# Running the first query block tile by tile at the head of a fused attention and gated-MLP kernel

**Chip, cores, metric.** One core of one Trainium2 chip. The metric is the device time of the program in microseconds (us); lower is better. Times are medians of several executions; most executions of one kernel agree within 0.3%. In the views PE is TensorE, PEld its weight loads, DVE VectorE, ACT ScalarE, and SPq the queue that issues DMAs; a block (or packet) of instructions is a piece of an engine's program that is fetched by DMA while the kernel runs.

## The reference

`x` is 2048 tokens by 512. Both branches read one layer-normalized `xn`, and the result is their sum with `x`.

```python
xn = (x - mean) / sqrt(var + 1e-5)
# A: sliding local attention, 32 heads of 16, a window of 8 keys two tokens apart
q, k, v = split(xn @ wqkv)
a = softmax(q . k[pos - 2*w] * 16**-0.5);  A = (sum_w a * v[pos - 2*w]) @ wo
# B: gated MLP with a spatial gate
z = gelu(xn @ w_in);  z1, z2 = z[:, :688], layernorm(z[:, 688:])
B = (z1 * (w_sp @ z2 + b_sp)) @ w_out
out = x + A + B
```

## The kernel before

Tokens come in 16 tiles of 128. Tile `i` belongs to block `i % 4`; block 0 is tiles 0, 4, 8, 12. To be of use to TensorE, a tile is loaded, its statistics taken on VectorE, the root on ScalarE, the tile normalized in place on VectorE, then transposed: by TensorE into PSUM and a copy (block 0, half of block 1) or by a DMA transpose (the rest). Below, "tile 0 to 3 of a block" counts within the block.

```python
load_x0(...); load_x(A, 0, 2, 4); load_wqk(SP, 0); load_x(SP, 1, 0, 2); load_wqk(SP, 1); ...   # all at the start

def ln_stats(i, parts=1):   # V.bn_stats, then V.bn_aggr
def ln_root(sl):            # A.activation(rstd, var, Abs_reciprocal_sqrt)
def ln_apply(i):            # V.tensor_scalar(x, x, mean, rstd, subtract, mult)

def tr(i):
    pt = ps_aux.tile([P, C, P], BF16, name="pt", tag="aux")          # four transposes in one PSUM tile
    for c in range(C):
        PE.transpose(pt[:, c, :], xall[:, j, tb, c * P:(c + 1) * P], ident[:])

def qk_part(pq, j, m, b0, b1, ccs=(0, 1), p0=None, kcs=range(C)):    # block j, tiles b0..b1 side by side
    for cc in ccs:
        for kc in kcs:
            PE.matmul(pq[:, cc, ...], wqk[:, sd, kc, c0 + cc:D:C], xv[:, kc, b0:b1, j, :],
                      start=(kc == 0), stop=(kc == C - 1))

# ---- prologue, cut
warm_up(10)
...                                            # tiles 0, 1 of block 0: statistics, roots, apply
tr_copy(t0[0], tr(t0[0]))
pt1 = tr(t0[1]); tr_copy(t0[1], pt1, 0, 2); tr_copy(t0[1], pt1, 2, 4)
warm_up(1); warm_up(1, 2)                      # filler matmuls
...                                            # tiles 2, 3: statistics, roots, then both applies
qk_part(pqs[0], 0, 0, 0, 2, kcs=range(2)) ...  # q, tiles 0 and 1 together, 256 columns a matmul
tr_copy(t0[2], tr(t0[2])) ...                  # tiles 2, 3: transposes
qk_part(pqs[0], 0, 0, 2, 4, ...) ...           # q, tiles 2 and 3 together
...                                            # k of block 0; tiles of block 1, two of them with tr_dma
load_x(SP, 3, 0, 4)
...                                            # q and k of block 1: first tiles 0 and 1, then tiles 2 and 3
ORDER = "z2.0 z1.3 p1.1 z2.2 zg2.0 p0.1 zg1.3 ..."   # the steady part, in a fixed order
```

The engines' orders are fixed by hand: each engine runs its instructions as the program names them.

Of the kernel before, what the change touches and what calls it, by code (L numbers as in the profile page):

```python
# [7 lines left out]
BF16 = mybir.dt.bfloat16  # L8
# [6 lines left out]
P = 128  # L15
S = 2048
D = 512
# [3 lines left out]
C = D // P  # L21
# [48 lines left out]
def kernel(  # L70
# [13 lines left out]
    V = nc.vector  # L84
    A = nc.scalar
    G = nc.gpsimd
    PE = nc.tensor
# [9 lines left out]
    ps_aux = ctx.enter_context(tc.tile_pool(name="ps_aux", bufs=2, space=PSUM))  # L97
# [4 lines left out]
    xall = r_x[:, 0:4 * TB * D].rearrange("p (j b d) -> p j b d", j=4, b=TB)  # L102
    vp = r_x[:].rearrange("p (d t) -> p d t", d=DH)
    r_w = sb.tile([P, 8192], BF16, name="r_w")
    wqk = r_w[:, 0:4096].rearrange("p (s k f) -> p s k f", s=2, k=C)
# [30 lines left out]
    xnT = sb.tile([P, C, S], BF16, name="xnT")  # L136
# [7 lines left out]
    ident = sb.tile([P, P], BF16, name="ident")  # L144
# [5 lines left out]
    stats = sb.tile([P, NT, 12], F32, name="stats")  # L150
# [21 lines left out]
    def load_x(E, j, b0, b1):  # L172
        for tb in range(b0, b1):
            E.dma_start(xall[:, j, tb], xblk[j][:, tb])
# [32 lines left out]
    def ln_stats(i, parts=1):  # L207
        j, tb = i % 4, i // 4
        w = D // parts
        for h in range(parts):  # L210
            V.bn_stats(stats[:, i, 6 * h:6 * h + 6], xall[:, j, tb, w * h:w * h + w])  # L211
        V.bn_aggr(mv[:, i, :], stats[:, i, 0:6 * parts])  # L212

    def ln_root(sl):
        A.activation(rstd[:, sl], mv[:, sl, 1], ACT.Abs_reciprocal_sqrt, bias=eps_t[:])

    def ln_apply(i):
        j, tb = i % 4, i // 4
        V.tensor_scalar(xall[:, j, tb, :], xall[:, j, tb, :], mv[:, i, 0:1], rstd[:, i:i + 1],  # L219
                        ALU.subtract, ALU.mult)  # L220

    def tr(i):
        j, tb = i % 4, i // 4
        pt = ps_aux.tile([P, C, P], BF16, name="pt", tag="aux")
        for c in range(C):
            PE.transpose(pt[:, c, :], xall[:, j, tb, c * P:(c + 1) * P], ident[:])
        return pt

    def tr_copy(i, pt, c0=0, c1=C):
        A.copy(xnT[:, c0:c1, i * P:(i + 1) * P], pt[:, c0:c1, :])  # L230

    def tr_copy_v(i, pt, c0, c1):
        V.tensor_copy(xnT[:, c0:c1, i * P:(i + 1) * P], pt[:, c0:c1, :])

    def tr_dma(i):
        j, tb = i % 4, i // 4
        SP.dma_start_transpose(xnT[:, :, i * P:(i + 1) * P], xall[:, j, tb, :])
# [57 lines left out]
    def qk_part(pq, j, m, b0, b1, ccs=(0, 1), p0=None, kcs=range(C)):  # L295
        sd, c0 = m // 2, 2 * (m % 2)
        p0 = b0 if p0 is None else p0
        xv = xnT[:].rearrange("p k (b j t) -> p k b j t", b=TB, j=4)
        for cc in ccs:
            for kc in kcs:  # L300
                PE.matmul(pq[:, cc, p0 * P:(p0 + b1 - b0) * P], wqk[:, sd, kc, c0 + cc:D:C],  # L301
                          xv[:, kc, b0:b1, j, :], start=(kc == 0), stop=(kc == C - 1))

    def qk_copy(pq, j, m, b0=0, b1=TB, p0=None):
        sd, c0 = m // 2, 2 * (m % 2)
        p0 = b0 if p0 is None else p0
        if sd == 0:
            dst = qs[:, j, c0:c0 + 2, b0 * P:b1 * P].rearrange("p c (b t) -> p c b t", b=b1 - b0)
        else:
            dst = ks[:, c0:c0 + 2, HALO:HALO + S].rearrange("p c (b j t) -> p c b j t", b=TB, j=4)[:, :, b0:b1, j, :]  # L310
        cast = A.copy(dst, pq[:, :, p0 * P:(p0 + b1 - b0) * P].rearrange("p c (b t) -> p c b t", b=b1 - b0))  # L311
        if sd == 1:
            for i in k_reads[j]:
                tc.declare_no_dep(cast.ins, i, reason="other token columns of the same rows")
            k_casts[j].append(cast.ins)

    def qk_tile():
        return ps_mm.tile([P, 2, TBS], F32, name="pq", tag="mm")

    def qk_mm(j, m):  # L320
        tiles["q", j, m] = qk_tile()
        qk_part(tiles["q", j, m], j, m, 0, TB)
# [220 lines left out]
    def blk(j):  # L543
        return [4 * tb + j for tb in range(TB)]

    def col(i):
        return slice(i, i + 1)
# [4 lines left out]
    def warm_up(n, b=4):  # L552
        for _ in range(n):
            PE.matmul(pwm[:, 0, 0:b * P].rearrange("p (a b) -> p a b", a=b), warm[:, 0:P],
                      warm[:, 0:P].unsqueeze(1).broadcast_to([P, b, P]), start=True, stop=True)

    t0, i1 = blk(0), blk(1)
    i2, i3 = blk(2), blk(3)
    warm_up(10)
    for n in range(2):  # L560
        ln_stats(t0[n], 2)
        ln_root(col(t0[n]))
    for n in range(2):
        ln_apply(t0[n])
    tr_copy(t0[0], tr(t0[0]))
    pt1 = tr(t0[1])
    tr_copy(t0[1], pt1, 0, 2)
    tr_copy(t0[1], pt1, 2, 4)
    warm_up(1)
    warm_up(1, 2)  # L570
    for n in range(2, 4):
        ln_stats(t0[n])
        ln_root(col(t0[n]))
    for n in range(2, 4):
        ln_apply(t0[n])
    pqs = [qk_tile() for _ in range(3)]
    qk_part(pqs[0], 0, 0, 0, 2, kcs=range(2))
    qk_part(pqs[0], 0, 0, 0, 2, kcs=range(2, 4))
    qk_part(pqs[1], 0, 1, 0, 2, (0,))
    tr_copy(t0[2], tr(t0[2]))  # L580
    qk_part(pqs[1], 0, 1, 0, 2, (1,), kcs=range(2))
    pt3 = tr(t0[3])
    qk_part(pqs[1], 0, 1, 0, 2, (1,), kcs=range(2, 4))
    tr_copy_v(t0[3], pt3, 0, 2)
    tr_copy(t0[3], pt3, 2, 4)
    qk_part(pqs[0], 0, 0, 2, 4, kcs=range(2))
    qk_part(pqs[0], 0, 0, 2, 4, kcs=range(2, 4))
    qk_part(pqs[1], 0, 1, 2, 4)
    ln_stats(i1[0])
    ln_root(col(i1[0]))  # L590
    ln_stats(i1[1])
    ln_root(col(i1[1]))
    qk_copy(pqs[0], 0, 0)
    ln_apply(i1[0])
    ln_apply(i1[1])
    qk_copy(pqs[1], 0, 1)
    qk_part(pqs[2], 0, 2, 0, 4)
    for n in range(2, 4):
        ln_stats(i1[n])
        ln_root(col(i1[n]))  # L600
    for n in range(2, 4):
        ln_apply(i1[n])
        tr_dma(i1[n])
    load_x(SP, 3, 0, 4)
    tr_copy(i1[0], tr(i1[0]))
    pq3 = qk_tile()
    qk_part(pq3, 0, 3, 0, 4, (0,))
    tr_copy(i1[1], tr(i1[1]))
    qk_part(pq3, 0, 3, 0, 4, (1,))
    qk_copy(pqs[2], 0, 2)  # L610
    qk_copy(pq3, 0, 3)
# [9 lines left out]
    pqs = [qk_tile() for _ in range(3)]  # L621
# [44 lines left out]
    for tok in ORDER.split():  # L666
        name = tok.rstrip("0123456789.")
# [31 lines left out]
```

## Time and profile before

| | before |
|---|---|
| median of 3 | 203.11 us (202.89 to 203.21) |
| profiled span | 201.2 us |
| TensorE busy | 196.0 us, 97% |
| TensorE's waits from 5 to 30 us | 0.5, 0.4 and 0.2 us |

The prediction shows the views of the kernel before, and reads them. Two lines more are wanted. The first is the chain of work that ended last, by engine; the second is from the timeline of VectorE, whose columns are start, length, engine, line, operation, output and input: its first product of q and k, with which the steady part begins.

```profile
PE 89%; DVE 5%; DMA 3%; ACT 1%; issue 1%
```

```profile
24.85 1.22 DVE L335 TENSOR_TENSOR r_pr<-r_qk 128x2048 bf16<-128x2048 bf16 x1
```

### The profile page before, as it was taken

What the parts mean: (1) busy time and instruction counts of PE and PEld (TensorE: products, weight loads), DVE (VectorE), ACT (ScalarE), POOL (GpSimd) and SP (SyncE); (2) the same over time, 40 slices, a digit from 0 to 9 for tenths busy, and PEclk for the clock granted to TensorE, in tenths of its full rate; (3) what the DMA queues carried; (4) which work ended last, traced back from release to release, by engine and by line L of the source; (5) the groups of instructions that cost most, each with busy time, mean ns of one, the idle gap of its engine ahead of it and who ended that gap; (6) DMA issues with size and microseconds to landing.
All of it is one profiled execution on the core that took longest, in us unless ns stands there. A gap on an engine that the chain in (4) does not pass through costs nothing.

```text
span 201.2 us, 4028 instructions
## 1 busy us (share of the span) xinstructions
PE 196.0 (97%) x1659; PEld 123.7 (62%) x1659; DVE 184.5 (92%) x248; ACT 104.5 (52%) x175; POOL 17.4 (9%) x14
## 2 busy tenths in 40 slices
PE   7898999999999999999999999999999999999994
PEld 2768855665566666666656666666544646664562
DVE  5896899999989999999979999999999999999715
ACT  3585998899999996363341513807502230331300
POOL 3000000499600000000000000000000000000000
PEclk9999999999999999999999999999999999999999
DMA  5977648980000095554266999199950199206864
GB/s 164 261 244 111 142 95 261 143 173 0 3 0 0 3 134 102 170 93 104 66 145 134 239 270 164 26 228 178 194 92 0 54 232 169 67 30 121 212 190 136
DMA packets 66562, 25.91 MB, mean 129 GB/s; under 512 B 56496, under 2 KB 66288, under 8 KB 66288
## 3 DMA queue, kind: packets, MB, share of 16 engines
q1 hardware_dynamic: 65824, 25.19, 58.5%
q10 hardware_dynamic: 720, 0.47, 0.7%
q8 instruction: 13, 0.21, 0.5%
q14 instruction: 5, 0.04, 0.1%
HBM read 10.13 MB, written 2.10 MB: 61 GB/s over the span
## 4 chain that ended last, share of the span: by engine, by line
PE 89%; DVE 5%; DMA 3%; ACT 1%; issue 1%
PE pg L444 37%; PE pz L243 19%; PE pq L301 10%; PE pv L405 7%; PE po L527 7%; PE po L497 6%; DVE stats L211 2%; DMA xnT<-r_x 2%; DMA r_x<-in_A_x_dram 1%; PE pa L527 1%; PE pl L355 1%; DVE r_pr L515 1%; PE po L506 1%; PE pb L497 1%; DVE r_x L219 1%; DVE mv L212 1%
## 5 line engine op out<-in xcount | busy, mean ns | idle before, releaser
L444 PE MATMUL pg<-z,r_qk 128*128 128x344 bf16 x448 | 66.8, 309 | 0.0
L444 PEld LDWEIGHTS <-r_qk 128*128 128x128 bf16 x448 | 43.7, 98 | 22.0 <-issue 0.4
L419 DVE TENSOR_TENSOR r_pr<-r_x,r_w 128x2048 bf16<-128x2048 bf16 x32 | 38.4, 1220 | 1.3 <-PE pl L355 1.0
L243 PE MATMUL pz<-w_z,xnT 128*128 128x344 bf16 x256 | 39.3, 310 | 0.0
L423 DVE TENSOR_TENSOR r_pr<-r_pr 128x2048 bf16<-128x2048 bf16 x28 | 33.9, 1219 | 0.8 <-DVE r_pr L423 0.5
L243 PEld LDWEIGHTS <-xnT 128*128 128x128 bf16 x256 | 24.9, 98 | 13.2 <-issue 0.4
L450 ACT ACTIVATE gs<-pg,b_col 128x688 bf16<-128x688 f32 x16 | 13.2, 833 | 35.4 <-PE pg L444 32.6
L301 PE MATMUL pq<-xnT,r_w 128*128 128x256 bf16 (+1 forms) x168 | 28.8, 324 | 0.8 <-DMA xnT<-r_x 0.5
L335 DVE TENSOR_TENSOR r_pr<-r_qk 128x2048 bf16<-128x2048 bf16 x24 | 27.8, 1218 | 0.5 <-ACT r_qk L311 0.5
L301 PEld LDWEIGHTS <-r_w 128*128 128x128 bf16 x176 | 19.2, 114 | 9.3 <-DMA xnT<-r_x 0.8
L641 POOL CAST b_col<-b 128x16 f32<-128x16 bf16 x1 | 15.4, 15356 | 35.1 <-DMA b<-in_B_b_sp_dram 35.1
L510 ACT CAST r_qk<-po 128x512 bf16<-128x512 f32 x10 | 5.6, 588 | 23.1 <-PE po L527 22.7
L311 ACT CAST r_qk<-pq 128x1024 bf16<-128x1024 f32 (+1 forms) x16 | 15.3, 986 | 3.2 <-PE pq L301 3.0
L292 ACT ACTIVATE r_uz<-pz 128x688 bf16<-128x688 f32 x16 | 11.7, 739 | 6.6 <-PE pz L243 6.5
L497 PE MATMUL po<-r_lg,r_pr 32*128 32x512 bf16 x192 | 14.5, 375 | 0.0
L405 PE MATMUL pv<-xnT,r_w 128*32 128x512 bf16 x256 | 14.2, 379 | 0.0
L527 PEld LDWEIGHTS <-r_uz 128*128 128x128 bf16 x85 | 8.0, 98 | 9.4 <-issue 1.1
L344 DVE TENSOR_TENSOR r_pr<-r_pr 128x4096 bf16<-128x4096 bf16 x6 | 13.7, 2286 | 0.0
L527 PE MATMUL po<-r_w,r_uz 128*128 128x512 bf16 x60 | 13.6, 380 | 0.0
L211 DVE BATCH_NORM_STATS2 stats<-r_x 128x6 f32<-128x512 bf16 (+1 forms) x18 | 10.8, 611 | 2.8 <-DMA r_x<-in_A_x_dram 2.8
L267 ACT ACTIVATE junk<-z 128x688 bf16<-128x688 bf16 x16 | 12.4, 774 | 0.1
L261 ACT ACTIVATE z<-pz 128x688 bf16<-128x688 f32 x16 | 11.8, 739 | 1.2 <-PE pz L243 1.2
(79 smaller groups left out, 185.2 us busy)
## 6 DMA issues: line engine op xcount, KB each, us to landing
r_lg<-in_A_wo_dram SPq DMA_DIRECT2D x8, 256.0 KB, 4.0
r_x<-in_A_x_dram SPq DMA_DIRECT2D x12, 128.0 KB, 3.1
out_dram<-r_qk SPq DMA_DIRECT2D x12, 128.0 KB, 3.6
r_w<-in_A_wqkv_dram SPq DMA_DIRECT2D x8, 128.0 KB, 3.5
r_qk<-in_A_x_dram SPq DMA_DIRECT2D x8, 128.0 KB, 2.5
w_z<-in_B_w_in_dram SPq DMA_DIRECT2D x4, 172.0 KB, 3.6
w_z<-in_B_w_in_dram SPq DMA_DIRECT2D x1, 688.0 KB, 6.9
r_w<-in_B_w_out_dram SPq DMA_DIRECT2D x1, 640.0 KB, 5.3
```

Of the source, the lines that this page charges most:

```text
L211: V.bn_stats(stats[:, i, 6 * h:6 * h + 6], xall[:, j, tb, w * h:w * h + w])
L243: PE.matmul(pz[:, hh, 0:FHALF], xnT[:, kc, i * P:(i + 1) * P], wz[:, kc, hh * FHALF:(hh + 1) * FHALF], start=(kc == 0), stop=(kc == C - 1))
L301: PE.matmul(pq[:, cc, p0 * P:(p0 + b1 - b0) * P], wqk[:, sd, kc, c0 + cc:D:C], xv[:, kc, b0:b1, j, :], start=(kc == 0), stop=(kc == C - 1))
L311: cast = A.copy(dst, pq[:, :, p0 * P:(p0 + b1 - b0) * P].rearrange("p c (b t) -> p c b t", b=b1 - b0))
L335: prod = V.tensor_tensor(pr[g % 3][:, c].rearrange("p w b t -> p b w t"), q3.unsqueeze(2).broadcast_to([P, TB, 4, P]), k4, ALU.mult)
L405: PE.matmul(pv[32 * tb:32 * tb + 32, dd, :], wv[:, kc, 2 * d2 + dd, :], xnT[:, kc, tb * TBS:(tb + 1) * TBS], start=(kc == 0), stop=(kc == ...
L419: V.tensor_tensor(pw_t[n], vp[:, :, off:off + P], a_sb[:, slot_w(w), ts].unsqueeze(1).broadcast_to([P, DH, P]), ALU.mult)
L423: V.tensor_tensor(pw_t[n] if dst is None else dst, pw_t[n], pw_t[m], ALU.add)
L444: PE.matmul(pg[:, hh, 0:FHALF], wsp[n][:, k, :], z2[:, k, hh * FHALF:(hh + 1) * FHALF], start=(k == 0), stop=(k == NT - 1))
L497: PE.matmul(pc, op[32 * tb:32 * tb + 32, d, o * P:(o + 1) * P], wo_r[32 * tb:32 * tb + 32, d, cs], start=(d == 8), stop=False, tile_positi ...
L527: PE.matmul(pc, uT[:, o % 2, m, tb * P:(tb + 1) * P], wout[:, m, cs], start=False, stop=(m == MCH - 3))
L641: G.tensor_copy(b_col[:], b16[:])
```

## The change

The intent: let q of block 0 begin as soon as one half of the first tile is transposed, and let nothing on its way stand behind work that can wait. q runs a tile at a time with the weight row outermost; so a tile needs only those rows of the transpose, and of the weights, that have arrived. Statistics, roots and copies are put in the order in which they are wanted; the transposes of tiles 2 and 3 go to two PSUM banks, so that ScalarE and VectorE can each copy one half. The core of the diff:

```diff
+    def tr2(i):
+        pts = [ps_aux.tile([P, 2, P], BF16, name="pt", tag="aux") for _ in range(2)]
+        for c in range(C):
+            PE.transpose(pts[c // 2][:, c % 2, :], xall[:, j, tb, c * P:(c + 1) * P], ident[:])
+        return pts
+    def tr_copy2(i, pts):
+        A.copy(xnT[:, 0:2, i * P:(i + 1) * P], pts[0][:])
+        V.tensor_copy(xnT[:, 2:4, i * P:(i + 1) * P], pts[1][:])
+    def q_tile(tb, kcs):
+        for kc in kcs:
+            for c in range(C):
+                PE.matmul(pqs[c // 2][:, c % 2, tb * P:(tb + 1) * P], wqk[:, 0, kc, c:D:C],
+                          xnT[:, kc, 4 * tb * P:(4 * tb + 1) * P], start=(kc == 0 and tb % 2 == 0), stop=(kc == C - 1 and tb % 2 == 1))
@@ prologue, cut
-    tr_copy(t0[0], tr(t0[0]))
...
-    warm_up(1)
-    warm_up(1, 2)
...
-    qk_part(pqs[0], 0, 0, 0, 2, kcs=range(2))
-    qk_part(pqs[0], 0, 0, 0, 2, kcs=range(2, 4))
-    qk_part(pqs[1], 0, 1, 0, 2, (0,))
...
+    warm_up(2, 1)
+    pqs = [qk_tile() for _ in range(3)]
+    ln_stats(t0[2])
+    ln_root(col(t0[2]))
+    tr_copy(t0[1], pts[1], 2, 4)
+    q_tile(0, (0, 1))
+    q_tile(0, (2,))
+    q_tile(1, (0, 1))
+    q_tile(0, (3,))
+    ln_bn(t0[3])
+    ln_apply(t0[2])
+    ln_agg(t0[3])
+    pt2 = tr2(t0[2])
+    q_tile(1, (2, 3))
...
+    q_tile(2, (0, 1))
+    pt3 = tr2(t0[3])
+    q_tile(2, (2, 3))
+    tr_copy2(t0[3], pt3)
+    q_tile(3, (0, 1))
+    q_tile(3, (2, 3))
...                       # roots, applies and transposes of block 1 reordered in the same way
```

More of the change, by code (lines that the diff above doesn't have):

```diff
@@ L211, in ln_stats, with ln_bn, ln_agg @@
             V.bn_stats(stats[:, i, 6 * h:6 * h + 6], xall[:, j, tb, w * h:w * h + w])
+        ln_agg(i, parts)
+    def ln_bn(i):
+        V.bn_stats(stats[:, i, 0:6], xall[:, i % 4, i // 4, :])
+    def ln_agg(i, parts=1):
         V.bn_aggr(mv[:, i, :], stats[:, i, 0:6 * parts])
@@ L230, in tr_copy @@
         A.copy(xnT[:, c0:c1, i * P:(i + 1) * P], pt[:, c0:c1, :])
-    def tr_copy_v(i, pt, c0, c1):
-        V.tensor_copy(xnT[:, c0:c1, i * P:(i + 1) * P], pt[:, c0:c1, :])
+    def tr2(i):
+        j, tb = i % 4, i // 4
+        pts = [ps_aux.tile([P, 2, P], BF16, name="pt", tag="aux") for _ in range(2)]
[5 more added lines that the diff above has]
+        V.tensor_copy(xnT[:, 2:4, i * P:(i + 1) * P], pts[1][:])
     def tr_dma(i):
@@ L564 @@
         ln_apply(t0[n])
-    tr_copy(t0[0], tr(t0[0]))
-    pt1 = tr(t0[1])
-    tr_copy(t0[1], pt1, 0, 2)
-    tr_copy(t0[1], pt1, 2, 4)
-    warm_up(1)
-    warm_up(1, 2)
-    for n in range(2, 4):
-        ln_stats(t0[n])
-        ln_root(col(t0[n]))
-    for n in range(2, 4):
-        ln_apply(t0[n])
-    pqs = [qk_tile() for _ in range(3)]
-    qk_part(pqs[0], 0, 0, 0, 2, kcs=range(2))
-    qk_part(pqs[0], 0, 0, 0, 2, kcs=range(2, 4))
-    qk_part(pqs[1], 0, 1, 0, 2, (0,))
-    tr_copy(t0[2], tr(t0[2]))
@@ L581 @@
-    qk_part(pqs[1], 0, 1, 0, 2, (1,), kcs=range(2))
-    pt3 = tr(t0[3])
-    qk_part(pqs[1], 0, 1, 0, 2, (1,), kcs=range(2, 4))
-    tr_copy_v(t0[3], pt3, 0, 2)
-    tr_copy(t0[3], pt3, 2, 4)
-    qk_part(pqs[0], 0, 0, 2, 4, kcs=range(2))
-    qk_part(pqs[0], 0, 0, 2, 4, kcs=range(2, 4))
-    qk_part(pqs[1], 0, 1, 2, 4)
+    pts = [tr(t0[n]) for n in range(2)]
+    tr_copy(t0[0], pts[0], 0, 2)
+    tr_copy(t0[0], pts[0], 2, 4)
+    tr_copy(t0[1], pts[1], 0, 2)
+    warm_up(2, 1)
+    pqs = [qk_tile() for _ in range(3)]
@@ L589 @@
+    ln_stats(t0[2])
[10 more added lines that the diff above has]
+    q_tile(1, (2, 3))
+    ln_root(col(t0[3]))
+    tr_copy2(t0[2], pt2)
+    ln_apply(t0[3])
+    q_tile(2, (0, 1))
[4 more added lines that the diff above has]
+    q_tile(3, (2, 3))
     ln_stats(i1[0])
@@ L590 @@
     ln_root(col(i1[0]))
+    qk_copy(pqs[0], 0, 0)
     ln_stats(i1[1])
     ln_root(col(i1[1]))
-    qk_copy(pqs[0], 0, 0)
+    qk_part(pqs[2], 0, 2, 0, 4, (0,))
     ln_apply(i1[0])
-    ln_apply(i1[1])
-    qk_copy(pqs[1], 0, 1)
-    qk_part(pqs[2], 0, 2, 0, 4)
-    for n in range(2, 4):
-        ln_stats(i1[n])
-        ln_root(col(i1[n]))
-    for n in range(2, 4):
-        ln_apply(i1[n])
-        tr_dma(i1[n])
+    qk_part(pqs[2], 0, 2, 0, 4, (1,), kcs=range(2))
+    pt = tr(i1[0])
+    qk_part(pqs[2], 0, 2, 0, 4, (1,), kcs=range(2, 4))
@@ L604 @@
+    ln_stats(i1[2])
+    qk_copy(pqs[1], 0, 1)
+    ln_root(col(i1[2]))
+    ln_apply(i1[1])
+    tr_copy(i1[0], pt)
+    ln_bn(i1[3])
+    ln_apply(i1[2])
+    tr_dma(i1[2])
+    ln_agg(i1[3])
+    ln_root(col(i1[3]))
+    ln_apply(i1[3])
+    tr_dma(i1[3])
     load_x(SP, 3, 0, 4)
-    tr_copy(i1[0], tr(i1[0]))
     pq3 = qk_tile()
-    qk_part(pq3, 0, 3, 0, 4, (0,))
-    tr_copy(i1[1], tr(i1[1]))
+    qk_part(pq3, 0, 3, 0, 4, (0,), kcs=range(2))
+    pt = tr(i1[1])
+    qk_part(pq3, 0, 3, 0, 4, (0,), kcs=range(2, 4))
@@ L609 @@
+    tr_copy(i1[1], pt)
     qk_part(pq3, 0, 3, 0, 4, (1,))
```

## The prediction

> **What bounds the kernel now.** I read the page first, then busy time by stretches, then the tensor engine's waits, then the timelines of PE and of the DMA-issuing queue from 5 to 30 us, and last the DMA traffic around the one long wait.
>
> ```profile
> span 201.2 us, 4028 instructions
> PE 196.0 (97%) x1659; PEld 123.7 (62%) x1659; DVE 184.5 (92%) x248; ACT 104.5 (52%) x175; POOL 17.4 (9%) x14
> ```
>
> TensorE is the bound. The table by stretches says where it is not:
>
> ```profile
> 5.38:9.25 3.87, 3.47 (x34) 2.73 (x34) 3.02 (x9) 2.23 (x7) 0.00 (x0) 1.00 0.93 250
> 9.25:19.16 9.91, 9.39 (x73) 7.42 (x73) 8.85 (x24) 7.10 (x14) 0.00 (x0) 1.00 0.75 185
> 24.85:40.00 15.15, 15.15 (x91) 9.17 (x89) 15.15 (x14) 13.10 (x27) 2.19 (x1) 1.00 0.79 168
> 40.00:80.00 40.00, 40.00 (x434) 25.19 (x433) 39.37 (x45) 36.71 (x68) 13.40 (x2) 1.00 0.31 52
> ```
>
> The second number of a row is PE's busy time. From 24.85 us it fills every stretch, and it goes on so up to the last few us: nothing is to be had there, and the diff touches nothing there. All that the change can win lies before 19.2 us. PE's waits between 5 and 30 us are three:
>
> ```profile
> PE pq L301 <- DMA xnT<-r_x: 0.5, 1, 0.5
> PE pt L226 <- DVE r_x L219: 0.4, 1, 0.4
> PE pq L301 <- DVE xnT L233: 0.2, 1, 0.2
> ```
>
> The middle one is before the first transpose and stays. Besides these, PE spends time on fillers:
>
> ```profile
> 6.11 0.49 PE L554 MATMUL pwm<-warm 128*128 128x512 bf16 x2
> 6.73 1.47 PE L301 MATMUL pq<-xnT,r_w 128*128 128x256 bf16 x12
> ...
> 8.04 0.39 PE L226 MATMUL pt<-ident,r_x 128*128 128x128 bf16 x4
> 8.26 0.38 PE L301 MATMUL pq<-xnT,r_w 128*128 128x256 bf16 x2
> ```
>
> The long wait is at 19.16, where q/k of block 1 needs its tiles 2 and 3, which come by DMA transposes. The chain of waits and the queue's timeline:
>
> ```profile
> 15.02 4.09 DMA xnT<-r_x
> 19.11 0.05 issue
> 19.16 3.69 PE pq L301 x32
> ```
>
> ```profile
> 13.62 2.60 SPq L237 DMA_TRANSPOSE xnT<-r_x  x2
> 16.27 3.15 SPq L174 DMA_DIRECT2D r_x<-in_A_x_dram  x4
> 19.52 10.36 SPq L237 DMA_TRANSPOSE xnT<-r_x  x8
> ```
>
> The second transpose takes 4.09 us; transposes of this line take 2.5 us as a rule (the page of DMA issues for the first 32 us). And the four loads behind it take 3.15 us to issue where six took 2.80 before. The DMA view of 16 to 18 us shows why:
>
> ```profile
> DMA  9000368999999989999990000000000010101000
> q1 hardware_dynamic: 514, 0.13, 87.8%
> q8 instruction: 1, 0.02, 5.1%
> ```
>
> One packet of instructions (16 KB; 5.1% of 16 engines for 2 us is 1.6 us of one engine) sits on one engine just when the transpose runs. Fifteen engines are through by 17.1 us; the sixteenth finishes about 18.4.
>
> **What the Trainium skill says.** (1) "Runtime: NRT & Kernel Launch", Instruction fetch mechanics: an engine's instructions come in 16 KiB blocks of 256, over a DMA queue of its sequencer. The trace agrees: that queue moved 13 packets, 0.21 MB, and the program has 3320 PE rows, 3320/256 = 13.0. (2) "TensorE: Matmul & The Clock Gate", Back-to-back issue gap: an isolated gap of N/2.4 + 2.5 ns, 56 ns for N=128, but some 81 ns sustained with weight loads. The trace has 8.26 - 8.04 = 0.22 us for four transposes of 128 columns with their own weights, 55 ns each, so I take 55 and keep 81 as a rival. (3) "PSUM — Partial Sum Buffer", the four PSUM rules: a matmul with the start flag clears the written bits of a whole bank, and of two groups open in one bank only the first may have it. That is why the new q sets it only on even tiles; it costs no time.
>
> **The change part by part.** Times are on the clock of the profile before. Durations from its rows: 128-column matmul 55 ns, 256 columns 109, 512 columns 216 (spacings); half transpose copy on ACT 0.37 us, cast 1.0, root 0.30 (the next starts some 0.1 earlier); bn_stats plus aggregate 0.79 per tile; apply 0.33 to 0.41.
>
> *q of block 0.* Old: 32 matmuls of 256 columns, the first held until both tiles 0 and 1 are copied (6.73). New: 64 of 128 columns, the same 3.5 us; tile 0 with weight rows 0 and 1 needs only the first half-copy. That copy now follows two transposes (about 5.70), done at 6.07, so q starts at about 6.2 instead of 6.73; the fillers shrink from 768 columns to 256. Weight rows land at 5.6, 6.5 and 7.1 by the releases in the trace, and the new order never asks earlier. Tile 2: root at 6.67 to 6.97 between the copies, apply 7.16 to 7.56 ahead of the aggregate of tile 3, transposes at 7.65, split copy on both engines to 8.35. Tile 3: root to 8.0, apply to 8.7, transposes at 8.8, both halves copied by 9.5. q then runs on to 10.4; before it ended at 11.03. So 0.6 us is won by here: the 0.2 wait, most of 0.5 us of filler and waiting at 6.1 to 6.7.
>
> *k of block 0, start of block 1.* ACT now stands in the way. Root of block 1 tile 0 at 10.4, q cast at 10.6, root of tile 1 at 11.5, second q cast at 11.7, root of tile 2 at 12.6, copy of tile 0 at 12.8, root of tile 3 at 13.7, copy of tile 1 at 13.9 to 14.45. PE, done with k at 14.3, starts block 1 at about 14.5 (before 14.93). Its second and third PSUM tiles follow the k casts at 15.4 and 16.3, so the part that needs tiles 0 and 1 ends at 17.2 + 0.9 = 18.1; before, 18.48.
>
> *The DMA transposes of tiles 2 and 3.* Applies at 13.15 to 13.55 and 14.0 to 14.4, before 13.2 to 13.6 and 13.6 to 14.0. The queue issues one per 1.4 us from 13.62, so both go out as now, 13.6 and 15.0. Alone, the reordering would win nothing at 19.1: the 0.4 would become a longer wait.
>
> *The block of instructions.* In the run before it comes when PE starts row 193, as if the sequencer were 64 rows ahead at 256. The new q has 32 more matmuls, 64 more rows, all earlier. Row 193 is then in the middle of k, at about 11.2 instead of 16.0. There it meets loads of x and of the z weights, which have slack (before they landed by 14.7; wanted at 14.4 for x of block 2, 21 for z). So my estimate for the transpose is 15.0 + 2.5 = 17.5, and PE starts the second half of block 1 at 18.1 instead of 19.16. The loads of block 3 and the transposes of block 2 go out 1.3 us earlier (18.2 instead of 19.5), so q of block 2, at 26.2 before and about 25.1 now, still finds its last tile (22.1 + 2.5 = 24.6). DVE ends the statistics of block 3 1.1 us earlier and starts products at 23.7 instead of 24.85.
>
> Sum: -1.05 us at 19 us, then carried by a PE without gaps to the end: 203.1 - 1.05 = 202.1. I add a little for what I have missed: 202.2.
>
> **Rivals.** (a) Head start lost at the DMA: the transpose lands at 19 as before, because the fetch moves less than I think, or its delay just reaches the transposes over a backlog. For: no apply comes earlier, and the fetch stops one ring for 1.6 us. Then 203.1, 0 to 0.2 us won. (b) Weight loads bound the short matmuls: 81 ns instead of 55 makes 64 x 26 = 1.7 us more for q. For: the strided weights' load lasts 114 ns against 98. Against: two such loads, at 8.21 and 8.65, took 0.17 us the pair, so they overlap. Block 1 would start at 15 to 15.5, and the gain fall to 0 to 0.5: 202.6 to 203.1. (c) All later fetches move 64 rows forward too and one meets a transpose that PE waits for, or DVE becomes the bound (0.8 us between its last apply add at 189.1 and PE's use of it at 189.9). PE had no such wait in 170 us with 12 fetches, so a small chance: up to 203.6.
>
> **Range and chances.** My own case gives 201.9 to 202.3, (a) and (b) 202.6 to 203.1, (c) above. Weights about 6:3:1; with run-to-run spread of 0.3 us the range is 201.4 to 203.1. A change of 2% is 4.1 us; PE's waits and fillers before 19.2 us sum to 1.5 us, so faster by 2% is all but excluded, and slower would need q to be wholly bound by something unseen: 0.01 each.
>
> **What would show it.** First q matmul near 6.2; 128-column matmuls at 55 ns; last q matmul near 10.4; the instruction packet near 11 and none at 16; the second transpose of block 1 landing near 17.5; the loads of block 3 issued in about 1.9 us; PE's wait for the transpose gone and matmuls of the second half starting near 18.1; first product on DVE near 23.7. I am wrong if the wait for the transpose is as long as before or longer, if q's spacing is 80 ns, or if PE has a new gap after 25 us.

## The result

| | before | after |
|---|---|---|
| median of 6 | 202.99 us (202.89 to 203.21) | 202.07 us (202.00 to 202.53) |
| ratio | | 0.9959, 95% interval 0.9946 to 0.9972 |
| profiled span | 201.2 us | 200.2 us |

The ratio is the mean time of the one kernel's runs over that of the other's of the same rounds, so not quite the ratio of the two medians. The change is 0.4 to 0.5% faster, clear of noise and well inside 2%. Four of its six runs lie between 202.00 and 202.09, two at 202.42 and 202.53; that will matter below.

The head of the profile page after, and the chain of work that ended last:

```profile
span 200.2 us, 4094 instructions
PE 195.9 (98%) x1691; PEld 124.1 (62%) x1691; DVE 184.5 (92%) x249; ACT 104.0 (52%) x176; POOL 18.5 (9%) x14
```

```profile
PE 95%; DVE 2%; DMA 1%; issue 0%; SPq 0%; ACT 0%
```

TensorE's busy time is the same to 0.1 us, with 32 matmuls more, and the span is 1.0 us shorter: what was taken out is time without work, and 512 columns of filler. VectorE and DMA have almost left the chain. Of TensorE's waits between 5 and 30 us, one is left:

```profile
PE pt L232 <- DVE r_x L225: 0.4, 1, 0.4
```

The timeline of TensorE to the middle of block 1 (start, length, what, how many merged):

```profile
6.13 0.28 PE L574 MATMUL pwm<-warm 128*128 128x128 bf16 x2
6.25 1.64 PE L321 MATMUL pq<-xnT,r_w 128*128 128x128 bf16 x24
...
9.13 1.57 PE L321 MATMUL pq<-xnT,r_w 128*128 128x128 bf16 x24
10.53 1.46 PE L315 MATMUL pq<-xnT,r_w 128*128 128x512 bf16 x6
...
18.08 0.38 PE L315 MATMUL pq<-xnT,r_w 128*128 128x256 bf16 x2
```

q starts at 6.25 instead of 6.73, and k follows at 10.53. From 9.13 to 10.53, 24 matmuls take 1.40 us, 58 ns each with one short hold among them. The second half of block 1, held to 19.16 before, starts at 18.08.

The queue that issues DMAs, from 13 us on:

```profile
13.59 2.61 SPq L251 DMA_TRANSPOSE xnT<-r_x  x2
16.25 2.00 SPq L174 DMA_DIRECT2D r_x<-in_A_x_dram  x4
18.35 10.91 SPq L251 DMA_TRANSPOSE xnT<-r_x  x8
```

The two transposes are issued as before (13.62 then, 13.59 now), but the four loads behind them take 2.00 us instead of 3.15, and the transposes of block 2 begin at 18.35 instead of 19.52. The DMA view from 16 to 18 us (the row of digits is the busy share of 40 slices of 0.05 us, in tenths):

```profile
DMA  0005569999999997431000000000043215878999
q1 hardware_dynamic: 708, 0.26, 53.6%
```

There is no packet of instructions here any more: the second transpose is through on all engines by 17.0, and from 17.5 the loads of block 3 run. The packet is found in the view from 12 to 14 us:

```profile
q8 instruction: 1, 0.02, 2.7%
```

2.7% of 16 engines for 2 us is 0.9 us of one engine; in the trace it starts at 12.55. VectorE's first product comes 1.1 us sooner than before:

```profile
23.77 2.35 DVE L355 TENSOR_TENSOR r_pr<-r_qk 128x2048 bf16<-128x2048 bf16 x2
```

### The profile page after: what moved, and what is told of

Read it like the earlier page. It is cut to its first block, busy times and chain, and to the rows that moved or that the text cites. A ratio compares the mean times of both kernels' runs of the same rounds, so it can differ in the third digit from the quotient of the medians.

```text
span 200.2 us, 4094 instructions
## 1 busy us (share of the span) xinstructions
PE 195.9 (98%) x1691; PEld 124.1 (62%) x1691; DVE 184.5 (92%) x249; ACT 104.0 (52%) x176; POOL 18.5 (9%) x14
## 4 chain that ended last, share of the span: by engine, by line
PE 95%; DVE 2%; DMA 1%; issue 0%; SPq 0%; ACT 0%
PE pg L464 37%; PE pz L257 19%; PE pq L315 12%; PE pv L425 7%; PE po L547 7%; PE po L517 6%; PE pq L321 2%; DMA r_x<-in_A_x_dram 1%; PE pa L547 1%; PE pl L375 1%; DVE r_pr L535 1%; PE po L526 1%; PE pb L517 1%; PE pa L315 0%; PE pt L232 0%
## 5 line engine op out<-in xcount | busy, mean ns | idle before, releaser
L315 PE MATMUL pq<-xnT,r_w 128*128 128x512 bf16 (+1 forms) x136 | 24.9, 335 | 0.0
L315 PEld LDWEIGHTS <-r_w 128*128 128x128 bf16 x144 | 15.9, 114 | 7.7 <-issue 0.6
L672 POOL CAST b_col<-b 128x16 f32<-128x16 bf16 x1 | 16.4, 16439 | 33.0 <-DMA b<-in_B_b_sp_dram 33.0
L517 PE MATMUL po<-r_lg,r_pr 32*128 32x512 bf16 x192 | 14.5, 375 | 0.0
L425 PEld LDWEIGHTS <-r_w 128*32 128x32 bf16 x256 | 9.5, 138 | 4.2
```

The source lines that it names most:

```text
L315: PE.matmul(pq[:, cc, p0 * P:(p0 + b1 - b0) * P], wqk[:, sd, kc, c0 + cc:D:C], xv[:, kc, b0:b1, j, :], start=(kc == 0), stop=(kc == C - 1))
L425: PE.matmul(pv[32 * tb:32 * tb + 32, dd, :], wv[:, kc, 2 * d2 + dd, :], xnT[:, kc, tb * TBS:(tb + 1) * TBS], start=(kc == 0), stop=(kc == ...
L517: PE.matmul(pc, op[32 * tb:32 * tb + 32, d, o * P:(o + 1) * P], wo_r[32 * tb:32 * tb + 32, d, cs], start=(d == 8), stop=False, tile_positi ...
L672: G.tensor_copy(b_col[:], b16[:])
```

## The experiments

Two theories. **F (fetch)**: more than half of the gain comes from the block of instructions, which in the kernel before met the second DMA transpose of block 1, and which 64 more rows of TensorE instructions bring forward to where it meets only loads that have time. **O (order)**: the gain comes from starting q earlier, and the fetch is a bystander. To move the fetch alone, empty TensorE instructions were put between the first warm-up matmuls. Each run has runs of the kernel before on the same chip beside it (medians 203.12 to 203.17). Every kernel gave a correct result.

| run | edit | us, median (range) | ratio to before |
|---|---|---|---|
| e1 | before + 64 empty | 203.98 (203.69 to 204.38) | 1.0037 |
| e6 | before + 32 empty | 202.46 (202.33 to 202.72) | 0.9969 |
| e8 | before + 16 empty | 202.52 (202.22 to 202.63) | 0.9968 |
| e4 | before + q tile by tile only | 202.02 (201.98 to 202.28) | 0.9940 |
| e2 | after, q in pairs of tiles | 203.99 (203.28 to 204.34) | 1.0031 |
| e7 | e2 + 32 empty | 203.02 (202.71 to 203.50) | 0.9997 |
| e5 | after, transposes in one bank | 202.09 (201.96 to 202.46) | 0.9943 |
| e9 | after + 32 empty | 202.39 (202.00 to 202.67) | 0.9960 |
| e12 | after, again | 202.27 (202.01 to 202.55) | 0.9956 |
| e10 | after, two z tiles exchanged | 201.92 (201.58 to 202.11) | 0.9941 |
| e11 | e4, two z tiles exchanged | 202.09 (202.00 to 202.28) | 0.9951 |

e1, e2, e4 and e5 ran on one chip, the rest on another. On the first, one of the eleven runs of the kernel before took 205.05, which lowers the four ratios by about 0.001; there the medians are the better measure.

### e1: the fetch moved alone, at a price

```diff
-    warm_up(10)
+    for _ in range(8):
+        warm_up(1)
+        pad(8)          # 8 empty PE instructions
+    warm_up(2)
```

> The kernel before with 64 empty PE instructions among the warm-up matmuls, nothing else. Theory F (fetch): the block of instructions is fetched at 11 to 13 us instead of 16.0, the second transpose of block 1 lands near 17.5 instead of 19.1, PE's wait of 0.5 us goes, the second half of block 1 starts at 18.5 to 18.6 instead of 19.16, and the total falls by 0.5 to 0.6 us, to about 202.4. Theory O (order): the gain comes from q starting earlier alone and the fetch is a bystander; then the transpose still lands at 19.1 and the total stays at 203.0. If the empty instructions cost PE time in the warm-up, the first transpose starts later than 5.4 and the test says less.

Measured: 203.98, slower by 0.8 us. An empty instruction takes 71 ns (one to the next in the trace), so eight of them are longer than the 0.43 us of a warm-up matmul, and TensorE came late to its first transpose:

```profile
1.06 5.87 PE L554 MATMUL pwm<-warm 128*128 128x512 bf16 x10 [1.06 <-DVE warm L189]
6.72 0.76 PE L226 MATMUL pt<-ident,r_x 128*128 128x128 bf16 x8
```

The fetch came at 13.00. The start is 1.34 us late (6.72 for 5.38) and the second half of block 1 starts at 19.95 for 19.16, only 0.79 late. TensorE's waits from 5 to 30 us:

```profile
PE pq L301 <- ACT xnT L230: 0.4, 1, 0.4
PE pq L301 <- DVE xnT L233: 0.2, 1, 0.2
```

The wait for the DMA transpose is gone. But with so late a start it might have gone anyway, so e1 settles nothing.

### e6 and e8: the same, small enough to be free

```diff
-        pad(8)
+        pad(4)          # e8: pad(2)
```

> The kernel before with 32 empty PE instructions, four behind each of eight warm-up matmuls; at the 71 ns that one took in the run with 64 they fit beside a warm-up matmul of 427 ns, so the first transpose should start at 5.4 as before. Theory F: the block of instructions comes 16 matmuls earlier, at about 14 us, the second transpose of block 1 lands near 17.5, the second half of block 1 starts at 18.5 to 18.6 instead of 19.16, total 0.5 to 0.6 below the kernel before. Theory O: 19.16 and the same total.

> The kernel before with 16 empty PE instructions: a half dose. Theory F: the block comes at about 15 us, in the middle of the first transpose of block 1; the engine that it holds is behind by some 1.6 us, so the second transpose lands between 17.7 and 18.5, just in time: total 0.3 to 0.6 below the kernel before. Theory O: no change.

Measured: 202.46 and 202.52. By the ratios that is 0.0031 x 203.1 = 0.63 us and 0.65 us less than the kernel before, for instructions that do nothing. The first transpose starts at 5.37 and 5.30, as before. The fetch came at 14.39 and 14.96 instead of 16.00. In e6, the packet in the DMA view from 14 to 16 us, the issuing queue, and TensorE at the second half of block 1:

```profile
q8 instruction: 1, 0.02, 2.9%
```

```profile
13.85 3.22 SPq L237 DMA_TRANSPOSE xnT<-r_x  x2
17.12 1.99 SPq L174 DMA_DIRECT2D r_x<-in_A_x_dram  x4
```

```profile
18.71 3.66 PE L301 MATMUL pq<-xnT,r_w 128*128 128x256 bf16 x32
```

TensorE's waits from 5 to 30 us are down to one:

```profile
PE pq L301 <- DVE xnT L233: 0.2, 1, 0.2
```

The block, now during the first transpose, delays the issue of the second a little (the two take 3.22 us to issue, before 2.60), but the second ends at 17.8, the loads behind it go out in 2 us, and TensorE does not wait. It starts the second half of block 1 at 18.71 (e8: 18.91); I had expected 18.5 to 18.6. The 0.2 that e6 misses lies in its prologue: q starts at 6.94 instead of 6.73. There TensorE still runs at half pace (transposes 107 ns apart, not 56) until about 6.7, in the kernel before only until about 4.3; this moment differs from profile to profile, without empty instructions too (e10: about 6.1). So F holds for this part, O does not: moving the fetch and nothing else in the order of work is worth 0.6 us (0.63, by the interval of the ratio 0.37 to 0.89). In the kernel before TensorE was ready for the second half at 18.48 and held to 19.16, so 0.68 was to be had.

### e4: q tile by tile alone

```diff
-    qk_part(pqs[0], 0, 0, 0, 2, kcs=range(2))
-    qk_part(pqs[0], 0, 0, 0, 2, kcs=range(2, 4))
-    qk_part(pqs[1], 0, 1, 0, 2, (0,))
+    q_tile(0, (0, 1))
+    q_tile(0, (2,))
+    q_tile(1, (0, 1))
+    q_tile(0, (3,))
...                     # and so on; statistics, roots, copies and banks as before
```

> The kernel before with q of block 0 tile by tile and weight rows outermost, but the old order of statistics, roots and copies and no split of the transposes over two banks. Theory F: 64 more PE rows, so the fetch moves as in the run with empty instructions, and the second half of block 1 starts near 18.5, total about 202.4 (0.3 to 0.4 above the whole change). Theory O: q itself starts hardly earlier (the first copy is still whole), so the total is 202.9 to 203.0.

Measured: 202.02, as good as the whole change (202.07), where I had expected 202.4. q still starts at 6.68, for the first copy is whole, but it no longer holds for tile 3: the wait of 0.2 us for VectorE's copy at 9.25 is gone, and TensorE has no wait left from 5 to 30 us in this run. (The 0.4 before the first transpose is filled by slower warm-up matmuls here; that transpose starts at 5.40, as before.) The fetch came at 12.05, and the second half of block 1 starts at 18.31:

```profile
18.31 3.66 PE L301 MATMUL pq<-xnT,r_w 128*128 128x256 bf16 x32
```

Against e6, which has the fetch out of the way too, that is 0.4 us less, by medians from two chips. By the traces tile by tile gives less: 18.31 against the 18.48 at which TensorE was ready in the kernel before is 0.17, the wait that went; the rest of the step from e6's 18.71 is the slow prologue of that profile.

### e2 and e7: the new order without tile by tile

```diff
-    q_tile(0, (0, 1))
-    q_tile(0, (2,))
-    q_tile(1, (0, 1))
-    q_tile(0, (3,))
+    qk_part(pqs[0], 0, 0, 0, 2, kcs=range(2))
+    qk_part(pqs[0], 0, 0, 0, 2, kcs=range(2, 4))
+    qk_part(pqs[1], 0, 1, 0, 2, (0,))
...                     # q of tiles 2 and 3 after both transposes; e7: and pad(4) as in e6
```

> The changed kernel with q of block 0 in pairs of tiles again (32 matmuls of 256 columns), new order of statistics and split transposes kept. q of tiles 2 and 3 must then wait for tile 3, so q ends near 11.4 instead of 10.5, and block 1 starts near 15.2 instead of 14.5. With 64 rows fewer the fetch comes back to 16 to 17.5 us. Theory F: it meets the second transpose of block 1 or the loads of block 3 again; the second half of block 1 starts at 19 or later, total 203.0 to 203.5. Theory O: the second half starts at 18.7, total 202.7.

> The changed kernel with q in pairs of tiles (as in the run of that name, which took 203.99) and 32 empty PE instructions. Theory F: the fetch moves from 16.7 to about 14.6, PE's waits for DMA transposes at 19.87 (0.2) and at 24.09 (0.5) go, total about 203.2 to 203.3. Theory O: the waits and 204.0 stay.

Measured: 203.99 and 203.02, where I had expected 203.0 to 203.5 and 203.2 to 203.3. With 64 rows fewer the fetch is back, at 16.71, and TensorE waits twice for DMA transposes; the two lines are from its waits from 5 to 30 us in e2, the third from the DMA view from 16 to 18.5 us:

```profile
PE pz L257 <- DMA xnT<-r_x: 0.5, 1, 0.5
...
PE pq L315 <- DMA xnT<-r_x: 0.2, 1, 0.2
```

```profile
q8 instruction: 1, 0.02, 4.0%
```

With 32 empty instructions more (e7) the fetch comes at 13.99, both waits are gone, and the time falls by 1.0 us, between medians from two chips (0.9 by the ratios, the outlier allowed for). This is the second pair of kernels that differ in empty instructions only, and F holds again, with a larger effect. e7 also shows that the new order without tile by tile is a loss: 203.02 against 202.46 of e6 on the same chip, since q of tiles 2 and 3 then waits for tile 3 with nothing between (0.3 us for its apply, 0.3 for its copy).

### e5: the split banks undone

```diff
-    pt2 = tr2(t0[2])
+    pt2 = tr(t0[2])
-    tr_copy2(t0[2], pt2)
+    tr_copy(t0[2], pt2)
...                     # tile 3 likewise, half on VectorE, then half on ScalarE
```

> The changed kernel with the transposes of tiles 2 and 3 in one PSUM tile again, copied by ACT whole (tile 2) and by VectorE and ACT one after the other (tile 3). Both theories: q waits 0.2 us longer for tile 2 and 0.3 for tile 3, q ends near 10.8, ACT's chain of roots and casts shifts by 0.2 to 0.3, so the second half of block 1 starts near 18.35 and the total is 202.3. If the shift is swallowed by ACT's waits for VectorE, 202.1.

Measured: 202.09, no different from 202.07. The profiled run (202.46, the slowest of its five) starts the second half of block 1 at 18.61, but part of that is a wait of 0.2 us for a weight row, which the first profile of the changed kernel does not have. By medians the split is worth less than the spread of runs; what may hide its worth is told under e9 and e12.

### e9 and e12: what the slower runs of the changed kernel have

```diff
-    warm_up(10)
+    for _ in range(8):
+        warm_up(1)
+        pad(4)
+    warm_up(2)
```

> The changed kernel with 32 empty PE instructions more. Theory F: the block comes at about 10.5 to 11 instead of 12.55, where only loads with slack run, so 202.0 to 202.1 as the changed kernel. If the total is higher by 0.3 or more, an early block is not free either (it holds back k weights or x of block 1).

> The changed kernel once more, on the same chip as the two next, as their measure: 202.0 to 202.1, with a run or two near 202.4 to 202.5 as before.

Measured: 202.39 and 202.27; the changed kernel again, on this chip, has three of six runs between 202.37 and 202.55. In e9 the fetch came at 10.27; its 0.12 us over e12 is within the spread, so whether so early a block costs anything stays open. The profiled runs of both belong to the slower ones, and both have a wait that the first profile of the changed kernel had not. In e12:

```profile
PE pz L257 <- DMA xnT<-r_x: 0.2, 1, 0.2
```

It is at 22.03 (e9: 0.5 us, at 22.43): the first z tile wants the first DMA transpose of block 2. In the first profile that transpose landed at 21.62 and z started at 21.67: no slack at all. The DMA view of e12 from 19.5 to 21 us has another packet of instructions, of 8 KB, on another queue:

```profile
q14 instruction: 1, 0.01, 1.8%
```

1.8% of 16 engines for 1.5 us is 0.43 us of one engine, at 20.16, in the midst of that transpose, which lands at 21.98.

The kept traces say more: every profile has such a packet near 20 to 22 us. In the six profiles of kernels with both the new order and the split (after, e2, e7, e9, e10, e12) it starts 1.4 to 1.8 us after that transpose was issued, and the transpose lands 3.3 to 3.9 us after its issue. In the other seven, e5 with the split undone among them, it starts 2.2 to 2.5 us after the issue, and the transpose lands after 2.6 to 2.7 us. So the first profile of the changed kernel has the collision too (packet at 19.76), and it is not confined to slow runs. The six have one VectorE instruction more than the seven (x249 for x248 on the page), the copy of the split, so the split may be what brings the packet forward; which engine's instructions these are is not shown.

### e10 and e11: the z tiles exchanged

```diff
-z2.0 z1.3 p1.1 z2.2 zg2.0 p0.1 zg1.3 ...
+z1.3 z2.0 p1.1 z2.2 zg1.3 p0.1 zg2.0 ...
```

> The changed kernel with the first two z tiles in the other order (tile 3 of block 1 first, tile 0 of block 2 second, and their gelus likewise). Theory S (second collision): the first transpose of block 2 lands at 21.6 in the changed kernel, just when PE wants it, and a block of 8 KB of instructions at about 20 us, whose moment varies, makes it late by up to 0.5 us in some runs. With 1.2 us more of slack the runs at 202.4 to 202.5 vanish and the median falls by 0 to 0.1 us, to 201.9 to 202.0. If the runs at 202.4 have another cause they stay, median 202.05.

> The kernel before with q tile by tile alone, as in the run of that name (202.02), and the same exchange of the two z tiles. Its second half of block 1 starts 0.2 us later than the changed kernel's, so if the new order of statistics and the split banks are worth anything, it is now 0.1 to 0.2 above the changed kernel with the exchange: 202.1. If they are worth nothing, the same, 201.9 to 202.0.

Measured: 201.92 for the changed kernel with the exchange, against 202.27 without on the same chip: none of its six runs is above 202.11, four of the other's six are. The transpose landed just as late, at 21.89, in the profiled run of e10, but TensorE has 1.2 us of other work first:

```profile
18.09 3.66 PE L315 MATMUL pq<-xnT,r_w 128*128 128x256 bf16 x32
21.59 2.64 PE L257 MATMUL pz<-w_z,xnT 128*128 128x344 bf16 x17
```

No idle time stands behind the second line, and TensorE has no wait left from 5 to 190 us. That the wait for the late transpose made the slower runs is shown by this, as far as six runs against six go (the intervals of the two ratios overlap), and by the waits in e9 and e12; that the 8 KB packet made it late fits all thirteen traces, but no run moved that packet alone. e10 is the fastest kernel (ratio 0.9941, interval 0.9927 to 0.9955; the 0.9940 of e4 is lowered by the outlier). e11, without the new order and the split, took 202.09, 0.17 us more: what these parts win at 18 us (18.09 against 18.35) appears to reach the end once the next wait is out of the way. The intervals of the two ratios overlap, so this is likely, not shown.

## Why the prediction was right

- *The total.* 202.2 predicted, 202.07 measured, inside 201.4 to 203.1. The profiled run won 1.08 us at the second half of block 1 (19.16 to 18.08), 1.06 predicted, so the mechanism carries the number; the slower runs among the six it did not foresee.
- *q's start and pace.* 6.2 predicted, 6.25 measured; 55 ns a matmul predicted, 55 to 58 measured. Rival (b) fell. q ended at 10.5 for 10.4.
- *Start of block 1 behind ScalarE.* 14.5 predicted, 14.51 in the trace; second half 18.1 predicted, 18.08 measured. The sum of ScalarE's roots, casts and copies carried this.
- *The reordering wins nothing at the transpose by itself.* Right: the transposes were issued at 13.59 and 15.00 as before. Rival (a) fell: the second was through by 17.0, and the wait went.
- *The fetch.* Right in kind and, by e6, e8 and e7 against e2, causal. Its moment was wrong: 11.2 predicted, 12.55 in the first profile and 11.34 in e12. The step that failed is the one that has it come when TensorE starts row 193: by count of records it was row 215 in the one run and 197 in the other, so the sequencer is not always 64 rows ahead. Nothing hung on it, as both moments lie before the transposes. (The 3320 TensorE rows are 3318 by the page, two for each of 1659 matmuls; the 13.0 stays.)
- *Shares.* The prediction added up 1.05 us. Measured apart, the fetch gives 0.63, and tile by tile 0.2 (traces) to 0.4 (medians of two chips) more. The prediction put the order and the split on the path as well; on medians they give nothing (e4 against the changed kernel), and perhaps 0.2 with the next wait removed. They do start the second half 0.23 us earlier (18.08 against e4's 18.31), but in all the kernels that have both the next transpose is late.
- *"A PE without gaps to the end".* This step was wrong in part. I checked the slack of the last transpose of block 2 and not of the first, which z wants sooner, and took 2.5 us for its flight where 3.3 were measured (18.35 to 21.62). In the two profiled runs that were slow it cost 0.2 and 0.5 us, a mild form of rival (c), though the packet that seems to stand in its way is on another queue than TensorE's.

## What to carry to other kernels

Where an engine with no gaps waits once for one DMA, look at what shared the DMA engines at that moment before moving compute: here a block of instructions held one of 16 engines for 1.6 us, and 16 empty instructions, placed where the engine had time, won more than half of what a rewrite of the prologue won. Here edits that added or took instructions before such a point moved the blocks, so an ablation can compare kernels with the blocks in different places; move the blocks alone as a control, and look at the blocks of every queue, not only of the engine that you edit. When a wait has been removed, ask which transfer is now wanted with no slack, and give it another tile's work to hide behind.

## What the Trainium skill lacked or had wrong

- "Runtime: NRT & Kernel Launch", Instruction fetch mechanics, calls the cost of crossing a 16 KiB boundary mostly hidden. It lacks that the block takes the same DMA engines as the program's transfers: it held one engine for 0.9 to 1.6 us, and a transpose meeting it took 4.09 us instead of 2.5, with the queue's next load taking 1.73 us to issue instead of 0.57. Moving it was worth 0.63 us. An 8 KB packet on another queue, met by a transpose, went with 3.3 to 3.9 us instead of 2.6 to 2.7.
- The same section says of when a block is fetched only that it is while the one before runs. By count of records, TensorE had started row 193 (before), 215 and 197 (two runs of the changed kernel): the moment moves by over 1 us from run to run of the same kernel.
- "TensorE: Matmul & The Clock Gate", Back-to-back issue gap, gives some 81 ns sustained for 128 columns with weight loads. Here 24 such pairs in a row took 58 ns each and the isolated figure of 56 ns was nearer, with weights read at a stride of four elements.
- No page that I read gives the cost of an empty instruction on TensorE's sequencer: 71 ns each here, so that eight between matmuls of 0.43 us held up the matmuls and four did not.
